# One block row of attention weights: scaled by GpSimd, or transposed against a diagonal of reciprocals

## The chip, the cores and the metric

The kernel runs on one core of a Trainium2 chip. The metric is device time in microseconds (us) of one launch. The engines are TensorE (PE in the profile; PEld is its weight load, which overlaps the products), VectorE (DVE), ScalarE (ACT), GpSimd (POOL) and SyncE (SP, which issues most of the DMAs). Three runs of the kernel before took 785.95, 785.86 and 784.82 us, with a median of 785.86 us.

## What is computed

The reference is an attention over 4 batches of 8 heads (32 heads, 576 positions, 64 wide), then a mixture layer with a convolution and a gate, then a second mixing layer. Cut to the part that the change touches:

```python
scores = scale * np.matmul(q, k.transpose(0, 1, 3, 2))
cum = np.cumsum(np.maximum(s, 0.0), axis=-1)
bias = -(cum[:, :, :, None] - cum[:, :, None, :])
scores = np.where(causal, -1000000000.0, scores + np.minimum(bias, 0.0))
scores = scores - np.max(scores, axis=-1, keepdims=True)
attn = np.exp(scores)
attn = attn / (np.sum(attn, axis=-1, keepdims=True) + 1e-09)
return np.matmul(attn, v).astype(np.float32)
```

## The kernel before

Each head's 576 query rows are cut into four blocks of 128 rows and one of 64 (two heads share one tile for those last rows). The weights of block i are a tile `P{i}` of 128 rows and 128(i+1) columns, because later keys are masked; the widest of the four, `P3`, has 512 columns. For a block, `scores` (L767) lets TensorE form the scores in PSUM, VectorE adds the mask and finds the extreme of each row (`top`, L701), ScalarE takes the exponential into `P{i}` and sums each row (`exps`, L718), VectorE adds 1e-9 to the sums and inverts them (L791, L792), and GpSimd multiplies the whole tile by the reciprocal of its row, in place (`normalise`, L726, its instruction at L729). `RECIP = (2, 3)` says that VectorE inverts the sums of blocks 0 to 2 together behind block 2, and that of block 3 by itself; GpSimd then runs the three tiles, and later `P3`.

The output needs the weights with keys on the partitions. So `transp` (L845) lets TensorE turn each 128 by 128 piece of a `P` tile into PSUM (L863), with the piece as the stationary operand and an identity as the moving one, in four groups a head: of three, five, four and three pieces. The first group reads blocks 0 and 1, and each of the other three reads blocks 2, 3 and 4 or a part of them. ScalarE copies a group from PSUM to SBUF (tile `th`, L384), and `av` (L872, its products at L889) multiplies it by the values of a pair of heads. Four of a head's fifteen pieces are of `P3`: two in the second group, one in the third, one in the fourth; within its group each of them stands between other pieces, never last. Over 32 heads that makes 480 pieces, 128 of them of `P3`.

The program also has ordinary fp32 products: `keep_busy` (L488) begins it with `BUSY` = 11 fp32 products of 128 by 128 into a tile that nobody reads, and the scores of heads 0 to 7 are fp32 products.

The heads run one after the other in `att_head`: the scores of head h are interleaved with the transposes of head h-1 and the `av` of the pair before. From the second batch on, the first mixture layer of the batch before (`m1_in`, tiles `h`, L933, and `m1_out`, tiles `y`, L975) is laid between the heads' work, and after some 350 us only the later layers are left (`ma`, L1228, and `my`, L1424).

The order of every engine's instructions is written out ahead of time by a planner (`Plan.order`): it simulates the engines with a cost for each operation and takes, at each step, the first operation in program order that is ready. A piece to be turned costs TensorE 109 ns in the plan, and a `normalise` of w columns costs GpSimd 37 + 0.834 w + 208 ns. A ring (`RINGS`) says how many buffers a tile has; `CAPS` says how many PSUM banks a kind of tile may hold at once (one for the groups of pieces, `pt`).

Of the kernel before, what the change touches and what calls it, by code (L numbers as in the profile page):

```python
# [8 lines left out]
F32 = mybir.dt.float32  # L9
# [5 lines left out]
ALU = mybir.AluOpType  # L15
# [51 lines left out]
OUT_AT = {0: "o11", 18: "o22", 22: "o21", 28: "o12"}  # L67
LAG2 = 6

RECIP = (2, 3)  # L70

SLACK = 400
LATER = 0.08
# [2 lines left out]

CAPS = dict(sc=3, pt=1, av=5, h=4, y=4, tp=2, t1=4, mh=1, ma=8, my=8, mx=2)

RINGS = dict(P=2, qk=2, vr=2, qkh=1, x=2, wf=2, xs=5, g=12, hh=3, c=3, x2=4, w64=2, mh=5, o=4, snap=2, tt=3)


def f32(ap):
# [257 lines left out]
def tile_attention_moe_mixer(  # L340
# [14 lines left out]
    nc = tc.nc  # L355
# [10 lines left out]
    def pool(n, fn, r, w, two=False, extra=125):  # L366
        return plan.op("POOL", ((280 if st.get("late") else 148) + n * 2.1) if two else (37 + n * 0.834 + extra), fn, r, w)

    def dma(nbytes, fn, r, w):
        return plan.op("SP", 640, fn, r, w, late=nbytes / 360)  # L370
# [5 lines left out]
    def pe(ns, fn, r, w):  # L376
        return plan.op("PE", ns, fn, r, w)

    def mm(n, m=128):
        return max(n / 2.4 + 3, m / 1.2)  # L380


    def hi_act(out, src, r, w, n):
        act(n, lambda: nc.scalar.copy(out(), src()), r, w)  # L384
# [14 lines left out]
    st = {}  # L399
# [14 lines left out]
    def ring(pool_, cls, count, shape, dtype, name, at={}):  # L414
        n = at[pool_, cls] = at.get((pool_, cls), -1) + 1
        return pool_.buf(f"{cls}{n % count}", shape, dtype, name)

    def bank(cls, name):
        b = Buf(banks, None, [128, 512], F32, name, [banks.opened])
        b.cls = cls  # L420
        banks.live.append(b)
        plan.banked.append(b)
        return b
# [8 lines left out]
    ap = Pool(plan, "ap", "right", after=[dec.opened])  # L432

    def one(pool_, name, shape, dtype):
        return pool_.buf(name, shape, dtype, name)

    ident = one(mx, "ident", [128, 256], F32)
# [6 lines left out]
    def early(name, at, shape, dtype, rows=128):  # L444
        n = 1
        for x in shape:
            n *= x
        axes = " ".join("abc"[: len(shape)])

        def view(t):  # L450
            v = t[:rows, at : at + n]
            if dtype != F32:
                v = v.bitcast(dtype)
            return v.rearrange(f"p ({axes}) -> p {axes}", **dict(zip("abc", shape)))

        return Part(ws, view, name)
# [17 lines left out]
    rk = early("rk", 0, (2, S), F32R, NH)  # L474
    qkFs = [ring(ap, "qkA", RINGS["qk"], [128, 2, S], F32, f"qkF_{i}") for i in range(2)]

# [4 lines left out]
    key = [cc]  # L481
# [9 lines left out]
    for t in qkFs:  # L491

        dve(2 * S, lambda t=t: nc.vector.memset(t[0:64], 0.0), [], [(t, "z"), (t, "r0"), (t, "r1")], True)
        for i in range(2):
# [5 lines left out]
                extra=0,  # L500
# [32 lines left out]
    for t in p4s:  # L533
        o = pool(64, lambda t=t: nc.gpsimd.memset(t[:, S:640], 0.0), [], [(t, "pad")], extra=0)
# [41 lines left out]
    def load_split(src, h, l, c, n, name, lo=lo_pool, slack=0):  # L576

        raw = ring(dec, "raw", RINGS["w64"], [128, 512], I64, f"raw_{name}")
        load = dma(n * 1024, lambda: nc.sync.dma_start(out=raw[:, :n], in_=src[:, c : c + n]), [], [raw])
        load.preds.add(st["rows", 2])  # L580
        load.slack = 3 * slack
        wf = ring(dec, "wf", RINGS["wf"], [128, 512], F32, f"wf_{name}")
        plan.bias = LATER
# [5 lines left out]
    def load_cw():  # L589
        raw = ring(dec, "raw", RINGS["w64"], [128, 512], I64, "raw_cw")  # L590
        dma(24576, lambda: nc.sync.dma_start(out=raw[:, :24], in_=cwU[:, :24]), [], [raw])
        decode64(cw, [cw], raw, 24)
        pool(24, lambda: nc.gpsimd.tensor_scalar(cw(), cw(), 2.0**-8, 1.0, ALU.mult, ALU.mult), [cw], [cw])

    def load_mixu():
        raw = ring(dec, "raw", RINGS["w64"], [128, 512], I64, "raw_mix")
        wf = ring(dec, "wf", RINGS["wf"], [128, 512], F32, "wf_mix")
        dma(163840, lambda: nc.sync.dma_start(out=raw[:, :160], in_=cwU[:, 24:184]), [], [raw])
        decode64(lambda: wf[:, :160], [wf], raw, 160)
        act(160, lambda: nc.scalar.mul(wf[:, :160], wf[:, :160], 2.0**-8), [wf], [wf])  # L600

        def u():
            return wf[:, :160].rearrange("p (a b) -> p a b", b=32)

        hi_dve(lambda: uhl[:, :, 0:32], u, [wf], [(uhl, 0)], 160)
        lo_dve(lambda: uhl[:, :, 32:64], u, lambda: uhl[:, :, 0:32], [wf, (uhl, 0)], [(uhl, 1)], 160)
# [16 lines left out]
    xs = {}  # L623
# [73 lines left out]
    def top(ps, rows, w, m0, into, before, r, wr):  # L697

        dve(
            w if before is None else w + 50,  # L700
            lambda: nc.vector.tensor_tensor_reduce(  # L701
                out=ps[:rows, :w],
                in0=ps[:rows, :w],
                in1=mask[:rows, m0 : m0 + w],
                scale=-0.125,
                scalar=3.0e38 if before is None else before(),
                op0=ALU.add,
                op1=ALU.min,
                accum_out=into(),
            ),  # L710
            [ps, mask, *r],
            [ps, wr],
        ).late = 60
# [12 lines left out]
    def normalise(t, w, r, key, keys):  # L726
        pool(
            w,
            lambda: nc.gpsimd.tensor_scalar(t[:, :w], t[:, :w], r(), 1.0, ALU.mult, ALU.mult),  # L729
            [key] + keys,  # L730
            keys,
            extra=208,
        )

    def products(h, ps, rows, q0, k0, w):
        d = st[h]

        def mms():
            for c, t in enumerate(d["qk"]):
                nc.tensor.matmul(  # L740
                    ps[:rows, :w],
                    lhsT=t[:, 0, q0 : q0 + rows],
                    rhs=t[:, 1, k0 : k0 + w],
                    start=c == 0,
                    stop=c == len(d["qk"]) - 1,
                )

        pe(16 + 1.88 * w if h in FS else 2 * mm(w, rows), mms, d["qk"], [ps])
# [18 lines left out]
    def scores(h, i):  # L767
        P, sm = st[h]["P"][i], st[h]["sm"]
        w = 128 * i + 128
        ps = bank("sc", f"sc{h}_{i}")  # L770
        products(h, ps, 128, 128 * i, 0, w)
        top(ps, 128, w, 384 - 128 * i, lambda: sm[:, i : i + 1], None, [], (sm, f"m{i}"))
        exps(
            lambda: P[:, :w],
            ps,
            128,
            w,
            lambda: sm[:, i : i + 1],
            lambda: sm[:, 4 + i : 5 + i],
            (sm, f"m{i}"),  # L780
            [P, (sm, f"s{i}")],
        )
        if i in RECIP:
            ns = range(max((x + 1 for x in RECIP if x < i), default=0), i + 1)
            ss = [(sm, f"s{n}") for n in ns]
            rs = [(sm, f"r{n}") for n in ns]

            def r():
                return sm[:, 8 + ns[0] : 9 + i]

            dve(2, lambda: nc.vector.tensor_scalar(r(), sm[:, 4 + ns[0] : 5 + i], 1e-9, None, ALU.add), ss, rs)  # L791
            dve(15, lambda: nc.vector.reciprocal(r(), r()), rs, rs)  # L792
            for n in ns:
                Pn = st[h]["P"][n]
                normalise(Pn, 128 * n + 128, lambda n=n: sm[:, 8 + n : 9 + n], (sm, f"r{n}"), [Pn])

    def scores4(h):
# [47 lines left out]
    def transp(h, g):  # L845
        d = st[h]
        pt = bank("pt", f"pt{h}_{g}")
        blocks, pos, off, cost = [], {}, 0, 0
        for j, i0, i1 in GROUPS[g]:
            pos[j] = off  # L850
            for i in range(i0, i1 + 1):
                rows = 128 if i < 4 else 64
                blocks.append((j, i, rows, off))
                off += rows
                cost += 109
        n = off

        def tr():


            for j, i, rows, o in reversed(blocks):
                turn = ident[:, 128:256] if i == 4 and h % 2 == 0 else ident[:, 0:128]
                nc.tensor.transpose(  # L863
                    pt[:, o + rows - 128 : o + rows], d["P"][i][:, 128 * j : 128 * j + 128], turn
                )

        pe(cost, tr, [ident] + [d["P"][i] for i in sorted({b[1] for b in blocks})], [pt])
        th = ring(ap, f"th{h % 2}_{g}", 1 if h % 2 or g > 1 else 2, [128, n], F32, f"th{h}_{g}")
        hi_act(lambda: th[:, :n], lambda: pt[:, :n], [pt], [th], n)
        d[f"g{g}"] = (th, pos)  # L870
# [48 lines left out]
    x2 = {}  # L919
# [566 lines left out]
    for c, n in ((0, 384), (512, 224)):  # L1486
        o = pool(n, lambda c=c, n=n: nc.gpsimd.memset(mask[:, c : c + n], 0.0), [], [(mask, c)], extra=0)
# [17 lines left out]
    def att_head(h):  # L1505
# [20 lines left out]
        if h < NH:  # L1526
            scores(h, 2)
# [41 lines left out]
    for h in range(NH + 1):  # L1569
        b, hh = divmod(h - 1, H)  # L1570
# [48 lines left out]
    blocks = [u_block(w2a, 0)]  # L1619
# [107 lines left out]
    for f in range(8):  # L1727
        tag, k, n = ("x2", RINGS["x2"], S) if f < 4 else (("xth", "xtl")[f % 2], 2, 512)
# [40 lines left out]
    for f in range(8):  # L1769
        a = raws[0, f, "11"]  # L1770
        b, c_, d = b12[f], b21[f], b22[f]
# [12 lines left out]
    for n in range(len(seq) + LAG2):  # L1784
        if n < len(seq):
            c, f, wn, yn, bk = seq[n]
# [87 lines left out]
```

## Time and profile before

| | kernel before |
|---|---|
| median of 3 runs | 785.86 us |
| the profiled execution | 784.83 us |
| its span on the core | 783.0 us |
| mean granted TensorE clock | 0.998 |
| busy: PE, PEld, DVE, ACT, POOL | 768.0, 718.9, 590.3, 526.6, 187.3 us |
| transposes of the `P` tiles on TensorE (L863) | 480, to 344 us of the span |
| multiplications of the `P` tiles on GpSimd (L729) | 144, 16 of them of the shared last rows |

How to read it: the span is the profiled execution from its first to its last instruction, and the remaining 1.8 us lie around it. A busy time is the union of an engine's instructions. TensorE's are pipelined, so one of them lasts longer than it keeps the next one waiting; the pace of a row of equal instructions is read from a merged line of the timeline (its length less that of one instruction, divided by one less than their count). A name such as `pt<-ident,P` is the tile written and the tiles read.

### The profile page before, as it was taken

Reading aid. Unit: us, or ns where it says so; the run is one execution under the profiler, and the core shown is the slowest. Engines: PE = TensorE matmul, PEld = TensorE weight load, DVE = VectorE, ACT = ScalarE, POOL = GpSimd, SP = SyncE. Lnnn points to the kernel's source line nnn. Section 1 sums busy time; section 2 is a strip of 40 time slices with the busy share of each in tenths; the row PEclk is TensorE's granted clock in tenths of the full one; section 3 lists DMA queues with packets and bytes.
Section 4 is the critical chain, followed back from the end, with each engine's and each line's share of the span. In section 5 each row is a group of like instructions: output and inputs, shape, how many; then the busy total and the mean of one; then the engine's idle time right before and its main releaser. Section 6 shows DMA issues by size and latency. Waiting matters only on the chain.

```text
span 783.0 us, 15927 instructions
## 1 busy us (share of the span) xinstructions
PE 768.0 (98%) x5370; PEld 718.9 (92%) x5370; DVE 590.3 (75%) x1471; ACT 526.6 (67%) x1329; POOL 187.3 (24%) x296
## 2 busy tenths in 40 slices
PE   8899899999999999999999999999999999999998
PEld 5568797999898998999999999999999999999998
DVE  6889797646856359547999876656698998988984
ACT  6889797857868488776768535455566676656542
POOL 5556463633447244350231000000000000000000
PEclk9999999999999999999999999999999999999999
DMA  6688766645556347435134457889666968467121
GB/s 162 194 228 203 183 161 171 163 117 111 154 133 142 85 105 235 106 108 170 62 115 144 147 166 230 264 255 298 210 208 214 313 195 277 149 198 227 41 82 60
DMA packets 77187, 132.83 MB, mean 170 GB/s; under 512 B 10033, under 2 KB 52401, under 8 KB 77105
## 3 DMA queue, kind: packets, MB, share of 16 engines
q1 hardware_dynamic: 77072, 131.81, 58.1%
q8 instruction: 42, 0.69, 0.4%
q14 instruction: 41, 0.33, 0.1%
q10 hardware_dynamic: 32, 0.00, 0.0%
HBM read 77.71 MB, written 33.10 MB: 142 GB/s over the span
## 4 chain that ended last, share of the span: by engine, by line
PE 85%; DVE 7%; DMA 3%; ACT 2%; issue 2%; POOL 1%; SPq 0%; DVEq 0%; POOLq 0%; ACTq 0%
PE ma_A L1228 16%; PE y L975 12%; PE h L933 12%; PE my_X L1424 11%; PE ma_S L1228 7%; PE sc L740 6%; PE pt L863 6%; PE my_Y L1424 5%; PE av L889 5%; PE my_Z L1424 2%; DMA qkA<-t 1%; PE tp L992 1%; DVE b L1363 1%; PE t L1011 1%; DVE w L393 1%
## 5 line engine op out<-in xcount | busy, mean ns | idle before, releaser
L975 PE MATMUL y<-gh,w1o 128*128 128x288 f32 x512 | 115.6, 301 | 0.5 <-DVE w1o L393 0.5
L1228 PE MATMUL ma_A<-u,W 128*128 128x288 f32 x720 | 105.9, 295 | 0.0
L1228 PEld LDWEIGHTS ma_A<-u,W 128*128 128x128 f32 x720 | 99.4, 188 | 0.1
L701 DVE CUSTOM_DVE_ANT_0 sc<-sc,mask 128x128 f32<-128x128 f32 (+2 forms) x144 | 69.2, 499 | 33.1 <-PE sc L740 29.7
L729 POOL TENSOR_SCALAR P<-P,sm 128x128 f32<-128x128 f32 (+3 forms) x128 | 73.4, 590 | 71.3 <-DVE sm L792 45.4
L975 PEld LDWEIGHTS y<-gh,w1o 128*128 128x128 f32 x512 | 85.7, 188 | 1.6 <-DVE w1o L393 0.8
L945 DVE SCALAR_TENSOR_TENSOR c<-h,cw,c 128x288 f32<-128x288 f32 x128 | 64.4, 512 | 29.1 <-ACT c L941 28.3
L396 POOL TENSOR_TENSOR gl<-c,gh 128x288 fp32r<-128x288 f32 x64 | 56.7, 890 | 111.5 <-ACT gh L960 103.5
L933 PE MATMUL h<-xh,w1h 128*128 128x290 f32 x256 | 79.4, 310 | 0.0
L1242 ACT COPY s<-ma_A 128x288 f32<-128x288 f32 x96 | 38.0, 399 | 58.3 <-PE ma_A L1228 38.4
L933 PE MATMUL h<-xl,w1h 128*128 128x290 f32 x256 | 76.7, 300 | 0.0
L933 PE MATMUL h<-xh,w1l 128*128 128x290 f32 x256 | 76.5, 299 | 0.0
L975 PE MATMUL y<-gl,w1o 128*128 128x288 f32 x256 | 75.3, 294 | 0.0
L718 ACT ACTIVATE P<-sc,sm 128x128 f32<-128x128 f32 (+3 forms) x128 | 68.1, 536 | 6.0 <-DVE sm L701 4.0
L384 ACT CAST w<-b 128x384 fp32r<-128x384 f32 x88 | 44.4, 514 | 37.8 <-PE my_X L1424 15.7
L384 ACT COPY th<-pt 128x384 f32<-128x384 f32 (+2 forms) x128 | 63.7, 499 | 8.1 <-PE pt L863 7.1
L1424 PE MATMUL my_X<-w,w 128*128 128x384 f32 x324 | 61.2, 335 | 0.1
L863 PE MATMUL pt<-ident,P 128*128 128x128 f32 x320 | 59.4, 273 | 0.4 <-DVE c L954 0.2
L1424 PEld LDWEIGHTS my_X<-w,w 128*128 128x128 f32 x324 | 56.5, 188 | 0.7 <-DVE w L393 0.4
L393 DVE TENSOR_TENSOR w<-b,w 128x384 fp32r<-128x384 f32 x88 | 47.3, 559 | 4.7 <-ACT w L384 3.3
L889 PE MATMUL av<-th,vr 128*64 128x320 f32 (+4 forms) x448 | 50.7, 363 | 0.0
L933 PEld LDWEIGHTS h<-xl,w1h 128*128 128x128 f32 x256 | 48.9, 191 | 1.0
(214 smaller groups left out, 1943.8 us busy)
## 6 DMA issues: line engine op xcount, KB each, us to landing
b<-ch_d SPq DMA_DIRECT2D x96, 192.0 KB, 3.6
ch_d<-s SPq DMA_DIRECT2D x64, 144.0 KB, 2.1
raw_w<-w_in SPq DMA_DIRECT2D x16, 512.0 KB, 4.8
raw_w2b<-w_in SPq DMA_DIRECT2D x16, 512.0 KB, 6.0
raw_w2a<-w_in SPq DMA_DIRECT2D x16, 512.0 KB, 5.5
t<-qk_in SPq DMA_DIRECT2D x24, 288.0 KB, 3.6
qkB<-t SPq DMA_DIRECT2D x24, 288.0 KB, 3.2
qkA<-t SPq DMA_DIRECT2D x24, 288.0 KB, 4.2
```

What stands on the lines that cost most here:

```text
L384: act(n, lambda: nc.scalar.copy(out(), src()), r, w)
L396: pool(n, lambda: nc.gpsimd.tensor_tensor(out(), src(), f32(hi()), ALU.subtract), r, w, two=True)
L701: lambda: nc.vector.tensor_tensor_reduce(out=ps[:rows, :w], in0=ps[:rows, :w], in1=mask[:rows, m0 : m0 + w], scale=-0.125, scalar=3.0e38 i ...
L718: lambda: nc.scalar.activation(out(), ps[:rows, :w], ACTF.Exp, bias=low(), scale=-1.0, accum_out=total()),
L729: lambda: nc.gpsimd.tensor_scalar(t[:, :w], t[:, :w], r(), 1.0, ALU.mult, ALU.mult),
L863: nc.tensor.transpose(pt[:, o + rows - 128 : o + rows], d["P"][i][:, 128 * j : 128 * j + 128], turn)
L889: nc.tensor.matmul(ps[64 * e : 64 * e + 64, o:n], lhsT=vr[:, e, j, :], rhs=t[:, pos[j] : pos[j] + w], start=c == 0, stop=c == len(ops) - 1 ...
L933: nc.tensor.matmul(ps[:, :W], lhsT=ww, rhs=xx, start=kt + n == 0, stop=kt == KT - 1 and n == 2)
L945: lambda k=k: nc.vector.scalar_tensor_tensor(c(), hh[:, k : k + HS], cw[:, 3 * f + k : 3 * f + k + 1], c(), ALU.mult, ALU.add),
L975: nc.tensor.matmul(ps[:, :HS], lhsT=ww, rhs=xx(), start=f + n == 0, stop=f == NF1 - 1 and n == 2)
L1228: nc.tensor.matmul(ps[:, :HS], lhsT=ww, rhs=uu, start=first and k == 0, stop=k == 5, skip_group_check=True)
L1424: nc.tensor.matmul(ps[:, :NC2], lhsT=ww, rhs=xx(), start=first and k == 0, stop=f == 7 and k == 2, skip_group_check=True,)
```

## The change

For block 3 alone, GpSimd no longer multiplies the 512 columns of `P3`. It multiplies the 128 columns of the identity by the reciprocals of the rows instead, into a new tile `dg` of 128 by 128 (one buffer in its ring), and leaves `P3` as the exponentials. TensorE then takes each of the four pieces of `P3` as the stationary operand against `dg` as the moving one in an ordinary fp32 product, where it took the identity in a transpose. The other blocks and their transposes stay as they are. The plan's cost of a piece is left at 109 ns.

```diff
-RINGS = dict(P=2, qk=2, ...)
+RINGS = dict(dg=1, P=2, qk=2, ...)
...
+    def diagonal(t, r, key):
+        pool(
+            128,
+            lambda: nc.gpsimd.tensor_scalar(t(), ident[:, 0:128], r(), 1.0, ALU.mult, ALU.mult),
+            [key, (ident, 0)],
+            [t],
+            extra=208,
+        )
...
             for n in ns:
                 Pn = st[h]["P"][n]
+                if n == 3:
+                    t = st[h]["dg"] = ring(ap, "dg", RINGS["dg"], [128, 128], F32, f"dg{h}")
+                    diagonal(t, lambda: sm[:, 11:12], (sm, "r3"))
+                    continue
                 normalise(Pn, 128 * n + 128, lambda n=n: sm[:, 8 + n : 9 + n], (sm, f"r{n}"), [Pn])
...
-                nc.tensor.transpose(
-                    pt[:, o + rows - 128 : o + rows], d["P"][i][:, 128 * j : 128 * j + 128], turn
-                )
-        pe(cost, tr, [ident] + [d["P"][i] for i in sorted({b[1] for b in blocks})], [pt])
+                dst, src = pt[:, o + rows - 128 : o + rows], d["P"][i][:, 128 * j : 128 * j + 128]
+                if i == 3:
+                    nc.tensor.matmul(dst, lhsT=src, rhs=d["dg"](), start=True, stop=True)
+                else:
+                    nc.tensor.transpose(dst, src, turn)
+        rows = sorted({b[1] for b in blocks})
+        pe(cost, tr, [ident] + [d["dg"]] * (3 in rows) + [d["P"][i] for i in rows], [pt])
```

## Rows read from the trace of the kernel before

**Rows 1.** The page, section 1: busy time and count of each engine.
```profile
PE 768.0 (98%) x5370; PEld 718.9 (92%) x5370; DVE 590.3 (75%) x1471; ACT 526.6 (67%) x1329; POOL 187.3 (24%) x296
```

**Rows 2.** The chain that ended last, whole span: shares by engine and line.
```profile
by line: PE ma_A L1228 16.3%; PE y L975 12.2%; PE h L933 11.7%; PE my_X L1424 11.2%; PE ma_S L1228 6.5%; PE sc L740 6.1%; PE pt L863 5.6%; PE my_Y L1424 5.3%; PE av L889 4.6%; PE my_Z L1424 2.1%; issue 1.5%; DMA qkA<-t 1.1%; PE tp L992 1.1%
```

**Rows 3.** Stretches of 25 us: busy us (count) of PE, PEld, DVE, ACT, POOL.
```profile
0.00:25.00 25.00, 22.05 (x120) 14.80 (x120) 18.23 (x59) 16.23 (x46) 11.91 (x37) 1.00 0.55 143
25.00:50.00 25.00, 22.40 (x139) 14.71 (x140) 21.74 (x72) 21.97 (x64) 15.31 (x21) 1.00 0.86 239
50.00:75.00 25.00, 25.00 (x184) 19.48 (x185) 21.02 (x70) 23.71 (x69) 14.60 (x22) 1.00 0.75 206
75.00:100.00 25.00, 21.66 (x152) 19.13 (x151) 20.38 (x56) 20.65 (x58) 12.29 (x16) 0.93 0.80 189
100.00:125.00 25.00, 24.10 (x180) 21.43 (x179) 23.21 (x72) 22.68 (x69) 12.67 (x16) 1.00 0.62 164
...
325.00:350.00 25.00, 25.00 (x198) 22.31 (x197) 9.44 (x30) 16.34 (x44) 11.38 (x21) 1.00 0.17 48
```

**Rows 4.** TensorE's groups by shape: busy us, mean ns of one, idle before them.
```profile
L863 PE MATMUL pt<-ident,P 128*128 128x128 f32 x320 | 59.4, 273 | 0.4 <-DVE c L954 0.2 <-issue 0.2
L863 PE MATMUL pt<-ident,p 128*128 128x128 f32 x160 | 38.0, 281 | 2.5 <-ACT th L384 1.9 <-ACT P L718 0.3
L488 PE MATMUL unread<-ws 128*128 128x128 f32 x22 | 4.4, 388 | 1.0 <-POOL ws L484 1.0
```

**Rows 5.** Timeline of the weight loads: start us, length us, what, count.
```profile
4.81 0.41 PEld L488 LDWEIGHTS unread<-ws 128*128 128x128 f32 x3
```

**Rows 6.** Weight loads of line 488: shortest, median and longest ns.
```profile
L488 PEld LDWEIGHTS unread<-ws x22: 192/333/333, 1.0 to 5.0; 128*128 128x128 f32 x22
```

**Rows 7.** Timeline of TensorE's products, columns as in rows 5.
```profile
14.17 0.46 PE L740 MATMUL sc<-qkF 128*128 128x128 f32 x2
14.46 0.38 PE L863 MATMUL pt<-ident,p 128*128 128x128 f32 x2
...
37.02 0.38 PE L863 MATMUL pt<-ident,P 128*128 128x128 f32 x2
...
62.29 0.27 PE L863 MATMUL pt<-ident,P 128*128 128x128 f32 x1
...
272.56 0.27 PE L863 MATMUL pt<-ident,P 128*128 128x128 f32 x1
```

**Rows 8.** GpSimd's groups by shape, columns as in rows 4.
```profile
L729 POOL TENSOR_SCALAR P<-P,sm 128x512 f32<-128x512 f32 x32 | 25.5, 797 | 2.9 <-ACT th L384 2.4 <-DVE sm L792 0.3
L729 POOL TENSOR_SCALAR P<-P,sm 128x128 f32<-128x128 f32 x32 | 13.1, 411 | 68.4 <-DVE sm L792 45.1 <-ACT th L384 10.9 <-ACT x L981 3.8
```

**Rows 9.** Timeline of GpSimd; merged lines end with a `P3`.
```profile
35.05 1.70 POOL L729 TENSOR_SCALAR P<-P,sm 128x256 f32<-128x256 f32 x3
40.80 0.74 POOL L729 TENSOR_SCALAR p<-p,sm 128x576 f32<-128x576 f32 x1 [4.05 <-ACT x L902]
...
59.66 2.14 POOL L729 TENSOR_SCALAR P<-P,sm 128x256 f32<-128x256 f32 x3
...
255.30 2.05 POOL L729 TENSOR_SCALAR P<-P,sm 128x128 f32<-128x128 f32 x4 [0.87 <-DVE sm L792]
```

**Rows 10.** Waits of the weight loads: us in total, times, longest us.
```profile
PEld pt L863 <- POOL P L729: 2.6, 5, 0.8
```

**Rows 11.** The chain in order of time: start us, length us, what.
```profile
72.58 8.78 DMA qkA<-t
...
115.55 1.64 POOL P L729
...
123.39 3.78 DMA raw_v<-mixV_in
...
245.98 0.69 POOL P L729
```

More of the change, by code (lines that the diff above doesn't have):

```diff
@@ L68 @@
 LAG2 = 6
-RECIP = (2, 3)
+RECIP = (2,3)
 SLACK = 400
@@ L77 @@
 CAPS = dict(sc=3, pt=1, av=5, h=4, y=4, tp=2, t1=4, mh=1, ma=8, my=8, mx=2)
-RINGS = dict(P=2, qk=2, vr=2, qkh=1, x=2, wf=2, xs=5, g=12, hh=3, c=3, x2=4, w64=2, mh=5, o=4, snap=2, tt=3)
+RINGS = dict(dg=1, P=2, qk=2, vr=2, qkh=1, x=2, wf=2, xs=5, g=12, hh=3, c=3, x2=4, w64=2, mh=5, o=4, snap=2, tt=3)
 def f32(ap):
```

## The prediction

> **What bounds the kernel now.** I read the page's busy times first, then the chain that ended last, then busy times by stretch, and only then the operations that the change touches. TensorE is busy for 768.0 of the 783.0 us of the span, GpSimd for 187.3 [rows 1]. The chain says the same: its ten largest entries are all TensorE's, and the transposes of this kernel, `PE pt L863`, hold 5.6% of it [rows 2]. The stretches show that this isn't so everywhere. In the first 125 us TensorE is idle for 2.95 + 2.60 + 0 + 3.34 + 0.90 = 9.8 us, while VectorE and ScalarE are close to as full as it is; at the end of the attention, 325 to 350 us, it has no idle time at all [rows 3]. So the reader should see an attention of some 345 us that is bound by TensorE, with a first third in which it shares that role. The change takes work from the engine with the most room and gives work to the one with none; what decides is the size of each and how much of each is on the chain.
>
> **What GpSimd gives up.** Per head it loses one multiplication of 512 columns and gains one of 128 columns of the same form. By the groups these take 0.80 and 0.41 us on average [rows 8]: 0.39 us a head, 12.3 us of GpSimd's time in all. Nearly none of it is on the path that sets the end. Set side by side head by head, the timelines of GpSimd and TensorE give the time from the end of `P3`'s multiplication to the first transpose that reads it. The shortest of the 32 is head 7's: GpSimd ends at 59.66 + 2.14 = 61.80 us [rows 9], the transpose starts at 62.29 [rows 7], 0.49 us later. The longest is head 25's: 257.35 [rows 9] against 272.56 [rows 7], 15.2 us. No wait of that kind exists in most heads; all waits of the weight loads of transposes for GpSimd's `P` tiles, blocks 0 to 2 among them, come to 2.6 us in five places [rows 10]. On the chain `P3` stands twice, with 1.64 us at 115.55 and 0.69 us at 245.98 [rows 11]; there it delays the next GpSimd operation, not a transpose. With 0.41 in its place that is worth 1.23 + 0.28 = 1.5 us. The gain is therefore between 0 (another operation is late next, such as the VectorE subtractions behind it) and 2.6 + 1.5 = 4.1 us; I take 1.5, since the chain names those two.
>
> **What TensorE takes on.** The piece of `P3` remains the stationary operand, so it is loaded as before; the product is fp32 without the transpose mode. The trace has such products of the same shape, 128 by 128 columns: the 11 that `keep_busy` issues at the start. They stand as 22 records, two weight loads and two matmuls for each product, where 320 + 160 records stand for 480 transposes, one for each [rows 4]. Price by the pace of the weight loads: three loads of the fp32 products last 0.41 us together [rows 5] and one lasts 0.19 [rows 6], so they follow each other after (0.41 - 0.19) / 2 = 0.11 us. Two transposes last 0.38 us together and one 0.27 [rows 7], so those follow each other after 0.11 us too. (Most loads of that line last 333 ns [rows 6] and are further apart; I use the settled last ones, since the transposes too run at the settled pace.) A product then costs 2 x 0.11 = 0.22 us where a transpose costs 0.11: 0.11 more for each of 128 pieces, 14.1 us of TensorE's time. Since a piece of `P3` always lies inside its group, a transpose follows it that can't start its load earlier, and no long product beside it can hide the second load. Bounds: less than 0.11 is excluded by the second load; the far end is the fp32 score product at 14.17 us, after which the next matmul starts 0.29 us later [rows 7], 0.18 more than a transpose, so 23.0 us in all. I take the near end, because that score product opened behind a wait and the pieces don't.
>
> Here a rule speaks louder against the change. In the rows, fp32 product and transpose differ by two loads against one. The Trainium skill, "TensorE: Matmul & The Clock Gate", section Terms, says that the transpose mode of trn2 is four times as fast for FP32; by that a product would cost 0.44 us, an estimate, and the change 42.2 us of TensorE's time instead of 14.1. The trace agrees with the direction only: records of either kind follow each other after 0.11 us, and the product has two of them, not four.
>
> **How much of it is on the path.** The chain holds 5.6% of 783.0 = 43.8 us of transposes [rows 2]; all 480 at 0.11 us are 52.8 us. So 83% of them are on the chain, and of 14.1 us added, 11.7 lengthen it if the order of the work stays. The other 2.4 us fall where TensorE waits for another engine, most of that in the first 125 us [rows 3]. Upper bound 14.1 (no cover at all), lower bound 8.4 (below).
>
> **What else moves.** The diagonal needs only the reciprocals and the identity, both there before. It has one buffer: GpSimd may write head h+1's only after TensorE has read head h's for the last time, in the fourth group. In ten of 31 heads the `P3` multiplication began before that read was over, by 0.1 to 1.2 us, 4.2 us together; the widest is head 4, whose multiplication was over at 35.05 + 1.70 = 36.75 us [rows 9], before head 3's last piece of `P3` was read, the first of the pair at 37.02 [rows 7]. GpSimd would now wait there with its queue behind it. What is queued in head 4's case is the multiplication at 40.80, which waits for ScalarE anyway [rows 9], so I cost this at nothing; without such cover it is 4.2 us. ScalarE's copy of a group starts 0.11 or 0.22 us later, which is in the 11.7 already. The planner sees cheaper GpSimd work and an unchanged cost of 109 ns for a piece, so it will write a somewhat different order for all engines, with TensorE 0.44 us a head slower than it thinks. I know no row for that; the nearest is TensorE's total idle time of 15.0 us [rows 1], of which a fifth either way, 3 us, is my estimate. I take zero.
>
> **The sum.** Against the profiled execution: 784.83 (span 783.0 and 1.83 around it) + 11.7 - 1.5 = 795.0 us. The median of the three runs lies 1.03 us above that execution, so on the median 785.86 + 10.2 = 796.1, rounded to 796.0 us.
>
> **Rivals.**
> - *The first heads hide theirs.* TensorE's idle time in the first 125 us [rows 3] takes up the 13 heads that run there: 13 x 0.44 = 5.7 us cost nothing, 19 x 0.44 = 8.4 stay, less 1.5: 792.8 us. For it: 9.8 us of idle time. Against: the transposes are on the chain in that stage too, between the waits, and idle time elsewhere in a head doesn't shorten a chain that runs through its transposes.
> - *New waits on top.* Nothing is covered (14.1 us), and the single `dg` buffer or the new order adds some 4 us: 804 us. For it: ScalarE and VectorE are nearly full in the first stage, and ten heads would wait. Against: GpSimd idles often, and most diagonals have microseconds to spare.
> - *Faster.* An earlier GpSimd brings the rounding of the next heads' `t` tiles forward (same queue, L387), and with it the transfers that TensorE waits for: the piece of 8.78 us at 72.58 on the chain and that of 3.78 at 123.39 [rows 11]. If both went wholly, 796.1 - 8.8 - 3.8 = 783.5 us. It decides only if these gains pass 10.2 us, so both have to go nearly whole. Against: the 8.78 us are the transfer and its queue, and 0.39 us a head is little beside that.
> - *Four passes at full price.* Each product takes four times a transpose, 0.33 us more for 128 pieces, 42.2 us, of which 83% are 35.1: 785.86 + 35.1 - 1.5 = 819.5 us. Against: two records at 0.11 us for each fp32 product [rows 4 to 6]. This is the rule of the Trainium skill weighed above.
> - *It doesn't do what it says.* The product against the diagonal runs at a transpose's price: only GpSimd's gain is left, 784.4 us. Against: the same two records.
>
> **How the numbers follow.** Chances: the forecast 0.62, with a range of its own from 793 to 800 (11.7 and 14.1, the gain from 0 to 4.1, an order worth up to 3 us in the likelier direction of each); first heads hidden 0.15; new waits 0.12; faster 0.04; four passes 0.03; no such price 0.04. About 0.2%, or 1.6 us, is what a measurement of this kernel can tell from no change. Slower by more: 0.62 + 0.15 + 0.12 + 0.03 = 0.92; within it (784.3 to 787.4): 0.04; faster: 0.04. The range has to take in the hidden case and half of the new waits to leave out less than 2 in 10: 790 to 804 us.
>
> **What would show it.** In the changed kernel's trace: 128 products `pt<-P,dg` as 256 records, their loads 0.11 us apart; 352 transposes; TensorE's record count up by 128; GpSimd's busy time down by some 12 us; the share of L863 on the chain up by some 10 us; the later layers, behind the attention, equally long but later by the whole difference. I am wrong if the loads of the products are closer or further apart than that, if the attention's end moves by less than 7 us (hidden) or more than 15 (new waits: look for GpSimd waiting for `pt`, or ScalarE's copies late), or if the waits of 8.78 and 3.78 us are gone.

## The result and the profile after

The changed kernel takes 796.02 us at the median, the kernel before 785.9 us beside it: 1.0116 times as long, 95% interval 1.0100 to 1.0132, which is 7.9 to 10.4 us more; the medians alone are 10.1 us apart. The forecast was 796.0 us. Its total held; two of its terms didn't, as the experiments show.

The page of the changed kernel, section 1, as in [rows 1]:

```profile
span 794.2 us, 16151 instructions
...
PE 780.3 (98%) x5498; PEld 732.2 (92%) x5498; DVE 588.5 (74%) x1471; ACT 529.3 (67%) x1329; POOL 179.0 (23%) x296
```

TensorE has 128 more records and 12.3 us more busy time, GpSimd 8.3 us less. The span grew by 11.2 us. The chain, as in [rows 2], has the transposes (L880) and the products (L878) on two lines now:

```profile
by line: PE ma_A L1244 16.1%; PE y L991 12.0%; PE my_X L1440 11.7%; PE h L949 11.4%; PE ma_S L1244 6.4%; PE sc L749 5.7%; PE my_Y L1440 5.5%; PE av L905 4.6%; PE pt L880 4.1%; PE pt L878 2.8%; PE my_Z L1440 2.1%; DMA qkA<-t 1.2%; issue 1.2%
```

Together they hold 6.9% of 794.2 = 54.8 us, where 5.6% of 783.0 = 43.8 us stood [rows 2]: 11.0 us more, nearly the whole growth of the span. Next, each line's instructions on the pieces (shortest, median, longest ns; first and last start in us):

```profile
L878 PEld LDWEIGHTS pt<-dg,P x256: 187/191/248, 13.2 to 353.4; 128*128 128x128 f32 x128
...
L880 PE MATMUL pt<-ident,P x192: 270/272/301, 11.9 to 353.7; 128*128 128x128 f32 x192
...
L880 PE MATMUL pt<-ident,p x160: 270/272/331, 13.2 to 353.3; 128*128 128x128 f32 x160
```

The 128 products are 256 records, and 352 transposes are left. The timeline of TensorE shows what one costs. These are the fourth groups of heads 12 and 31 in the kernel before (start us, length us, what, count):

```profile
126.14 0.27 PE L863 MATMUL pt<-ident,p 128*128 128x128 f32 x1
126.24 0.38 PE L863 MATMUL pt<-ident,P 128*128 128x128 f32 x2
...
343.22 0.27 PE L863 MATMUL pt<-ident,p 128*128 128x128 f32 x1
343.33 0.38 PE L863 MATMUL pt<-ident,P 128*128 128x128 f32 x2
343.46 0.38 PE L975 MATMUL y<-gh,w1o 128*128 128x288 f32 x1
```

and the same groups in the changed kernel:

```profile
127.57 0.27 PE L880 MATMUL pt<-ident,p 128*128 128x128 f32 x1
127.68 0.39 PE L878 MATMUL pt<-dg,P 128*128 128x128 f32 x2
127.90 0.27 PE L880 MATMUL pt<-ident,P 128*128 128x128 f32 x1
...
353.33 0.27 PE L880 MATMUL pt<-ident,p 128*128 128x128 f32 x1
353.44 0.39 PE L878 MATMUL pt<-dg,P 128*128 128x128 f32 x2
353.66 0.27 PE L880 MATMUL pt<-ident,P 128*128 128x128 f32 x1
353.69 0.38 PE L991 MATMUL y<-gh,w1o 128*128 128x288 f32 x1
```

From the first product record to the transpose behind it are 353.66 - 353.44 = 0.22 us, where a transpose takes 0.11. The same lines date the loss. Head 12's group begins 127.57 - 126.14 = 1.4 us late, head 31's 353.33 - 343.22 = 10.1 us. The 19 heads between add 8.7 us, 0.46 each, the full price of four products (0.44); the 13 heads before add 1.4 us, of the 5.7 that theirs cost, though two executions differ there by more than that, as a run below shows. Behind the last group 439.5 us were left before (783.0 - 343.46) and 440.5 are left after: that stretch has no part in it beyond what runs differ by.

### The profile page after: what moved, and what is told of

It is laid out like the page before. It is cut to its first block, busy times and chain, and to the rows that moved or that the text cites. A ratio compares the mean times of both kernels' runs of the same rounds, so it can differ in the third digit from the quotient of the medians.

```text
span 794.2 us, 16151 instructions
## 1 busy us (share of the span) xinstructions
PE 780.3 (98%) x5498; PEld 732.2 (92%) x5498; DVE 588.5 (74%) x1471; ACT 529.3 (67%) x1329; POOL 179.0 (23%) x296
## 4 chain that ended last, share of the span: by engine, by line
PE 86%; DVE 6%; DMA 3%; ACT 3%; issue 1%; POOL 1%; SPq 0%; DVEq 0%; POOLq 0%; ACTq 0%
PE ma_A L1244 16%; PE y L991 12%; PE my_X L1440 12%; PE h L949 11%; PE ma_S L1244 6%; PE sc L749 6%; PE my_Y L1440 6%; PE av L905 5%; PE pt L880 4%; PE pt L878 3%; PE my_Z L1440 2%; DMA qkA<-t 1%; PE tp L1008 1%; PE t L1027 1%; DMA qkF<-cc 1%
## 5 line engine op out<-in xcount | busy, mean ns | idle before, releaser
L729 POOL TENSOR_SCALAR P<-P,sm 128x128 f32<-128x128 f32 (+2 forms) x96 | 48.9, 526 | 68.6 <-DVE sm L801 38.6
L949 PEld LDWEIGHTS h<-xh,w1h 128*128 128x128 f32 x256 | 48.5, 189 | 0.6
```

What stands on the lines that cost most here:

```text
L949: nc.tensor.matmul(ps[:, :W], lhsT=ww, rhs=xx, start=kt + n == 0, stop=kt == KT - 1 and n == 2)
```

## Experiments

Each experiment's ratio goes to the runs of the kernel before on the same chip (785.1 to 785.7 us at the median); a difference in us is the ratio's.

**TensorE's part alone.** GpSimd and every engine's order stay those of the kernel before; only the four pieces of `P3` become products, against the identity.

```diff
-                nc.tensor.transpose(pt[...], d["P"][i][...], turn)
+                if i == 3:
+                    nc.tensor.matmul(dst, lhsT=src, rhs=turn, start=True, stop=True)
+                else:
+                    nc.tensor.transpose(dst, src, turn)
```

> TensorE's part alone: the 128 pieces of P3 go through ordinary fp32 products against the identity, GpSimd still multiplies all 512 columns, and the order of all engines is that of the kernel before. My theory (0.11 us more for each piece, 83% of it on the path, GpSimd's gain 1.5 us): 785.9 + 11.7 = 797.6 us, 1.5 us over the changed kernel. Rival, first heads hide theirs: heads 0 to 12 cost nothing and heads 13 to 31 pay 76 x 0.11 = 8.4 us, so 794.3 us, and the changed kernel would then have lost some 2 us elsewhere. Rival, no cover at all: 785.9 + 14.1 = 800.0 us.

Measured: 795.06 us, ratio 1.0127 (1.0111 to 1.0143), 10.0 us more (8.7 to 11.2). That is the whole loss of the change, with no change to GpSimd or to the order. The 11.7 us of the forecast lie just outside the interval, and full price (14.1) far outside.

**The first 13 heads alone, and the other 19.** The condition becomes `i == 3 and h < 13`, then `i == 3 and h >= 13`.

> As the run with all products, but only for heads 0 to 12 (52 pieces, 5.7 us of TensorE's time); the other heads keep transposes. If 83% of every head's price is on the path: +4.7 us, 590.6 + 200 = 790.6 us. If the share follows the chain of the kernel before head by head (28 of these 52 pieces lie on it): +3.1 us, 789.0 us. If the first heads hide theirs: no change, 785.9 us.

("590.6 + 200" is a slip of the pen; 785.9 + 4.7 is meant.) Measured: 788.01 us, ratio 1.0039 (1.0022 to 1.0056), 3.1 us more (1.7 to 4.4). Of a price of 5.7 us that is 54% (30% to 77%). Neither a free first stage nor the 83% of the forecast lies in the interval.

> As the run with all products, but only for heads 13 to 31 (76 pieces, 8.4 us of TensorE's time). If 83% of every head's price is on the path: +6.9 us, 792.8 us. If these heads pay in full, as the chain of the kernel before has it (73 of the 76 pieces lie on it): +8.0 to +8.4 us, 793.9 to 794.3 us.

Measured: 793.41 us, ratio 1.0098 (1.0083 to 1.0113), 7.7 us more (6.5 to 8.9), of a price of 8.4 us. Both expectations lie in the interval. The heads' starting times decide for the full price; these are the fourth groups of heads 12 and 31 in this run:

```profile
124.48 0.27 PE L867 MATMUL pt<-ident,p 128*128 128x128 f32 x1
...
349.96 0.27 PE L867 MATMUL pt<-ident,p 128*128 128x128 f32 x1
```

Between them lie 349.96 - 124.48 = 225.48 us, where the kernel before has 343.22 - 126.14 = 217.08: 8.4 us more, the full price of the 75 products between. The first 13 heads of this run are those of the kernel before, in the same order, and yet head 12's group begins 126.14 - 124.48 = 1.7 us earlier. So what the first heads cost can't be read from one pair of executions; the 1.4 us above are no measure of it, and the runs' ratios are.

**Is the cover a fixed stock?** The first 13 heads again, with each product issued twice.

```diff
                 if i == 3 and h < 13:
+                    for _ in range(2):
                     nc.tensor.matmul(dst, lhsT=src, rhs=turn, start=True, stop=True)
```

> As the run with products in heads 0 to 12 alone, but each of these 52 products is issued twice, so that a piece costs 0.33 us more than a transpose and the 13 heads 17.2 us of TensorE's time instead of 5.7. If a fixed share of the price lies on the path (54%, the share of these pieces on the chain of the kernel before): +9.3 us, 794.6 us. If the cover is a fixed stock of idle time, some 3 us: +14.2 us, 799.5 us.

Measured: 793.49 us, ratio 1.0105 (1.0089 to 1.0121), 8.2 us more (7.0 to 9.5), or 48% of a price of 17.2 us. So three times the price still costs about half of it: the cover grows with the price, as it does where some of the work lies beside the chain, and isn't a stock of some 3 us of idle time that is used up. In the first 125 us, where TensorE is busy for 115.2 us before [rows 3], it is busy for 120.69 us here, by this run's table of stretches (columns as in [rows 3], with the clock, the DMA share and GB/s behind them):

```profile
0.00:125.00 125.00, 120.69 (x854) 98.12 (x855) 97.20 (x301) 100.53 (x279) 63.56 (x108) 1.00 0.65 177
```

Which of the waits in that stage take up the other half was not singled out.

TensorE's clock is a rival for this cover. In the profiled execution of the kernel before, a stretch less than 2 us behind a wait of 1.81 us for the transfer of 8.78 us has the lower of the two levels, 1.2 GHz (the clock is the third number from the end):

```profile
83.20:86.40 3.20, 2.86 (x11) 2.26 (x10) 3.18 (x10) 3.00 (x11) 0.81 (x1) 0.50 0.85 172
```

The changed kernel's profile has no such stretch in the attention: its clock is 1.00 from 75 to 100 us. Runs with a mean clock of 0.999 or more leave this out: six of the kernel before, on the three chips of these runs, take 784.8 us on average, five with products in the first 13 heads 787.5 us, and all four with each product twice 793.4 us. That is 2.7 and 8.6 us more, again about half of either price, so the clock doesn't explain the cover.

**GpSimd's part alone.** The changed kernel, in its own order, with the pieces of `P3` transposed against the identity, so that block 3's weights are left undivided.

```diff
-                    nc.tensor.matmul(dst, lhsT=src, rhs=d["dg"](), start=True, stop=True)
+                    nc.tensor.transpose(dst, src, turn)
```

> GpSimd's part alone, in the order that the planner writes for the changed kernel: GpSimd makes the diagonal in place of the 512 columns, and TensorE transposes the pieces of P3 against the identity, so block 3 is left without its reciprocals and GpSimd doesn't wait for TensorE to read the diagonal. My theory: 785.9 - 1.5 = 784.4 us. Rival, GpSimd's time is worth nothing: 785.9 us. Rival, the new order itself costs: above 787.5 us.

Measured: 785.76 us, ratio 1.0002 (0.9991 to 1.0013), from 0.7 us less to 1.0 us more. The gain of 1.5 us isn't there. This is that run's chain in order of time (start us, length us, what), to be read beside [rows 11]:

```profile
113.51 0.16 DVE sm L800
...
116.17 1.10 POOL t L387
117.27 1.36 POOL dg L738
118.64 0.65 POOL t L387
...
123.36 5.15 DMA raw_v<-mixV_in
```

The piece of 1.64 us at 115.55 [rows 11] was to become 0.41 us. The diagonal takes 1.36 us there, though it has a quarter of the columns, behind a rounding of 1.10 us that the chain before doesn't have at this place. The transfer that ends the stretch starts at 123.36 us, where it started at 123.39 before. But this execution came into the stretch some 0.6 us later, by VectorE's addition to the sums (113.51 us); in the kernel before it stands at

```profile
112.89 0.16 DVE sm L791
```

So about half of the 1.23 us may have been saved by then. The transfer itself takes 5.15 us instead of 3.78, and it isn't shown that the change made it longer: this execution took 786.4 us, above its run's median, and in the runs with all products and with those of the other 19 heads, where GpSimd does what it did before, the same transfer takes 3.56 and 4.25 us. What the run shows is the sum: over the whole kernel nothing is gained.

Most diagonals are no dearer than 128 columns of the weights. In the changed kernel, by shape (busy us, mean ns, idle before):

```profile
L738 POOL TENSOR_SCALAR dg<-ident,sm 128x128 f32<-128x128 f32 x32 | 15.8, 493 | 16.0 <-PE pt L880 6.0 <-DVE sm L801 2.9 <-issue 2.7
...
L729 POOL TENSOR_SCALAR P<-P,sm 128x128 f32<-128x128 f32 x32 | 13.9, 436 | 68.6 <-DVE sm L801 38.6 <-ACT th L384 20.3 <-ACT x L997 3.8
```

The mean of 493 ns comes of a few long ones. The diagonals by themselves (shortest, median, longest ns; first and last start in us):

```profile
L738 POOL TENSOR_SCALAR dg<-ident,sm x32: 369/374/1222, 11.5 to 347.7; 128x128 f32<-128x128 f32 x32
```

In the kernel before, the 32 multiplications of 128 columns of weights have a median of 373 ns too, with a mean of 411 [rows 8].

**The wait for the single diagonal.** The diagonal's line by shape has it: GpSimd waited 6.0 us for TensorE. A second buffer needs room, so the tile of running sums moves into a free corner of the weight buffer; the control has that move alone.

```diff
-    cc = one(ap, "cc", [NH, S], F32)
+    cc = early("cc", 2000, (S,), F32, NH)
-RINGS = dict(dg=1, ...)
+RINGS = dict(dg=2, ...)
```

> A control for the run with two diagonals: the changed kernel, but the tile of running sums of s (2304 bytes a partition) lies in a corner of the weight buffer that is free at that time, which makes room in SBUF; nothing else changes, and the diagonal has one buffer. All theories: as the changed kernel, 796.0 us (10 us over the kernel before).

> The control with two buffers for the diagonal, so that GpSimd needn't wait for TensorE to have read the diagonal of the head before (in the changed kernel it waited ten times, 6.0 us together). My theory: what waits behind it in GpSimd's queue waits for something else anyway, so no change, 796.0 us, within 1 us of the control. Rival, the single buffer is part of the loss: up to 6.0 us faster, down to 790 us.

Measured: the control 793.93 us, ratio 1.0119 (1.0100 to 1.0137); two diagonals 794.78 us, ratio 1.0130 (1.0111 to 1.0149). The diagonal's line by shape, in the control:

```profile
L738 POOL TENSOR_SCALAR dg<-ident,sm 128x128 f32<-128x128 f32 x32 | 15.8, 494 | 15.6 <-PE pt L880 5.8 <-DVE sm L801 2.9 <-issue 2.4
```

and with two buffers:

```profile
L738 POOL TENSOR_SCALAR dg<-ident,sm 128x128 f32<-128x128 f32 x32 | 15.1, 471 | 5.3 <-DVE sm L801 4.2 <-DMA t<-qk_in 0.6 <-PE y L991 0.4
```

5.8 us of waits are gone and the time isn't less. The wait cost nothing that these runs can measure; from the two intervals it could be some 1.2 us at most, not 6.0.

**An order planned with the real price.**

```diff
-                cost += 109
+                cost += 218 if i == 3 else 109
```

> The changed kernel, but the planner is told that a piece of P3 costs TensorE 218 ns in place of 109, so the order of all engines is planned with the real price. My theory: the loss is TensorE's time itself and not a bad order, so within 1 us of the changed kernel's 796.0 us. Rival, the order planned with too low a price is part of the loss: 793 us or less, 3 us or more gained.

Measured: 794.46 us, ratio 1.0122 (1.0107 to 1.0136), the same as the changed kernel's to within some 2 us, so the 3 us of the rival are out. That the new order as a whole cost nothing fits the first run, which has the old order and the whole loss.

**One load for each product.** `P3` and the diagonal in fp32r, the format of the kernel's other products, so block 3's weights and reciprocals are rounded to it.

```diff
-ring(ap, "dg", RINGS["dg"], [128, 128], F32, f"dg{h}")
+ring(ap, "dg", RINGS["dg"], [128, 128], F32R, f"dg{h}")
-[ring(ap, f"P{i}_", ..., [128, 128 * (i + 1)], F32, f"P{g}_{i}") for i in range(4)]
+[ring(ap, f"P{i}_", ..., [128, 128 * (i + 1)], F32R if i == 3 else F32, f"P{g}_{i}") for i in range(4)]
```

> The changed kernel, but P3 and the diagonal are written in the reduced fp32 format (fp32r) that the kernel's other products use, so that the product is one weight load and one matmul in place of two; block 3's weights and reciprocals are thereby rounded to that format. Order and waits stay those of the changed kernel. My theory (the loss is the second load and matmul of each product): the price of 0.11 us is gone, as with transposes: 785.7 to 786.5 us, no change against the kernel before. Rival, the loss comes from the waits for the diagonal and from the new order: 796 us stays. Rival, half: a product costs more than a transpose even with one load: between 788 and 794 us.

Measured: 783.72 us, ratio 0.9983 (0.9973 to 0.9994). With one load and one matmul for each product the loss is gone (which of the two records sets the price isn't separated), and a little more: this is faster than both kernels, by 0.5 to 2.1 us on the kernel before, at the price of the rounding. TensorE's timeline of a second group in this kernel:

```profile
171.28 0.27 PE L880 MATMUL pt<-ident,p 128*128 128x128 f32 x1
171.30 0.31 PE L878 MATMUL pt<-dg,P 128*128 128x128 f32 x1
171.44 0.30 PE L880 MATMUL pt<-ident,p 128*128 128x128 f32 x1
171.50 0.31 PE L878 MATMUL pt<-dg,P 128*128 128x128 f32 x1
171.64 0.29 PE L880 MATMUL pt<-ident,P 128*128 128x128 f32 x1
```

and of one in the kernel before:

```profile
217.04 0.27 PE L863 MATMUL pt<-ident,p 128*128 128x128 f32 x1
217.15 0.27 PE L863 MATMUL pt<-ident,P 128*128 128x128 f32 x1
217.26 0.27 PE L863 MATMUL pt<-ident,p 128*128 128x128 f32 x1
217.37 0.38 PE L863 MATMUL pt<-ident,P 128*128 128x128 f32 x2
```

Five pieces start within 0.36 us here (171.28 to 171.64) and within 0.44 us there (four steps of 0.11). Whose gain the shorter time is, a run with TensorE's part alone tells: fp32r products against an fp32r copy of the identity, GpSimd multiplying all 512 columns, the tile of running sums moved as in the control.

> TensorE's part of the run with one-load products, alone: GpSimd multiplies all 512 columns as in the kernel before (and rounds P3 to fp32r), and the pieces of P3 go through fp32r products against an fp32r copy of the identity; the tile of running sums lies in the weight buffer to make room, as in the control. My theory: the gain of that run (1.4 us on the kernel before) is TensorE's, since GpSimd's part alone was worth nothing and its trace has a transpose and the product behind it start 0.17 us apart from the next pair instead of 0.22: 783.5 to 784.5 us. Rival, the gain came from GpSimd after all: 785.1 to 786 us, no gain here.

Measured: 783.5 us, ratio 0.9980 (0.9967 to 0.9993). The gain is TensorE's; GpSimd's part is again worth nothing. The fourth groups of heads 12 and 31 in this run, with the product behind the second:

```profile
126.20 0.27 PE L868 MATMUL pt<-ident,p 128*128 128x128 f32 x1
...
341.44 0.27 PE L868 MATMUL pt<-ident,p 128*128 128x128 f32 x1
341.46 0.31 PE L866 MATMUL pt<-idr,P 128*128 128x128 f32 x1
341.61 0.29 PE L868 MATMUL pt<-ident,P 128*128 128x128 f32 x1
341.66 0.38 PE L978 MATMUL y<-gh,w1o 128*128 128x288 f32 x1
```

From one group to the other are 215.24 us against 217.08: 1.8 us less for 75 products, some 0.02 us each. The starts inside a group promise more (three within 0.17 us against 0.22), but part of it is given back behind the group, where `y` starts 0.05 us after the last transpose and not 0.02. Carrying it further:

```diff
+                elif (j, i) == (0, 1):
+                    nc.tensor.matmul(dst, lhsT=src, rhs=idr(), start=True, stop=True)
...
+            if g == 2:
+                turns[1], turns[2] = turns[2], turns[1]
```

> The run with one-load products, carried further: in the first group of a head the middle of its three transposes also becomes an fp32r product (block 1 against an fp32r identity, block 1's weights rounded), and in the third group the product is put between the transposes, where it stood third of four. My theory, that a one-load product between transposes is some 0.02 us cheaper than a transpose: 32 to 64 such places, 0.7 to 1.5 us under the run with one-load products (783.7), 782.2 to 783.0 us. Rival, no more to be had: 783.7 us or above.

Measured: 784.24 us, ratio 0.9979 (0.9962 to 0.9996). Against the run before this is no change, and the 0.7 to 1.5 us that were expected are too little for these runs to confirm or to exclude.

## Why the prediction was right, and where it was not

- *The price of a product, 0.11 us more than a transpose:* right. It reads 0.22 us against 0.11 in the changed kernel; 19 heads pay 0.46 us each for four of them. The far end (0.18 us more) and the rival of four times a transpose are out, and so is that of a product at a transpose's price as long as it needs two loads.
- *The share on the path, 83%:* too high. TensorE's part alone cost 10.0 us (8.7 to 11.2) of 14.1, some 70%, where the sum had 11.7. Two steps failed. The share was taken from times: the chain of the kernel before goes through 372 of the 480 pieces, 78%, but stays with each for 0.118 us on average, so that 43.8 us divided by a pace of 0.11 make 83%. And one share was spread over all 32 heads and all 15 pieces of a head, where some half of the price lands on the path in the first 13 heads (54% and 48% in two runs) and all of it in the other 19 (8.4 us by their starting times). Counting only the pieces of `P3` that the chain goes through, 28 of 52 and 73 of 76, would have given 3.1 + 8.0 = 11.1 us, inside the interval.
- *GpSimd's gain, 1.5 us:* wrong, it is nil (at most 0.7 us). The sum took a long piece on the chain and replaced it by the mean of another shape; in its place the shorter operation took 1.12 to 1.36 us, and the run with GpSimd's part alone shows nothing left of the saving (785.76 us against 785.68). The lower bound, 0 because another operation is late next, was the better value.
- The two errors, 1.7 and 1.5 us, cancelled: that the total came out so close is luck, while its sign and size are not. The rival "first heads hide theirs" was half right in its mechanism: they hide half, and as a share, not as a stock. The rival "faster" is out: on the changed kernel's chain both transfers are there, and longer in this execution:

```profile
73.96 9.76 DMA qkA<-t
...
124.24 4.54 DMA raw_v<-mixV_in
```

- *The single diagonal and the order, at nothing:* right. Ten waits were forecast and ten came, 6.0 us together rather than 4.2, and taking them away or planning with the real price changed nothing that the runs can tell.
- *GpSimd's busy time, 12 us less:* 8.3 us. The diagonals, with their few long ones, take 15.8 us where `P3` took 25.5, which is 9.7 us less; GpSimd's other operations took the remaining 1.4 us more.

In the changed kernel's chain of the first stretch the diagonal stands with 1.12 us:

```profile
118.15 1.12 POOL dg L738
119.27 1.15 POOL t L387
```

## What to carry to other kernels

Before work is moved from an idle engine to TensorE, count the records of the new operation and their pace, and ask of each stage whether that engine's work lies on the chain there: the price is paid in full where it does, and in part elsewhere. Time saved on an engine that hardly anyone waits for can be worth nothing, as here, even where one of its operations stands on the chain: ask what starts earlier for it. If scaling is to be folded into a transpose, a product with a single load cost no more here than the transpose, where the precision allows it.

## What was not expected of the hardware

A single-load fp32r product of 128 by 128, put between two fp32 transposes, is cheaper than a transpose: a transpose, product, transpose, product and transpose start within 0.36 us, five transposes within 0.44 us, and the kernel gains 0.2%, some 0.02 us for each product after what is given back behind the group. Why the two kinds overlap better than one of them with itself wasn't tried. And the same GpSimd operation on 128 columns takes 0.37 us at the median but up to 1.22 us in one execution (the diagonal, changed kernel); no run here separates what makes the long ones long.
